# Second mixture, layer two: copies of the first two products moved ahead of operand halves on ScalarE, and one sum ahead of a low part on VectorE

## The chip, the cores and the metric

One core of a Trainium2 chip runs the whole program in one launch. The metric is device time in microseconds (us). An engine here is TensorE (PE in the rows), its weight load (PEld), VectorE (DVE), ScalarE (ACT), GpSimd (POOL) or SyncE (SP). The kernel was run three times; the profile below is of a further execution.

## The reference, cut to what matters

Attention within clusters feeds a first feed-forward block, and its output x (1536 tokens by 512) goes into a mixture of eight experts. The change touches only the mixture:

```python
logits = x @ w_gate
logits = logits - logits.max()
P = np.exp(logits)
for _ in range(8):
    P /= P.sum(1, keepdims=True) + 1e-09
    P /= P.sum(0, keepdims=True) + 1e-09
    P *= N / E
out = np.zeros((N, D), dtype=np.float32)
for e in range(E):
    h = np.maximum(x @ w1[e], 0.0)
    ye = h @ w2[e]
    out += P[:, e:e + 1] * ye
```

N is 1536, D 512, E 8, and w1[e] is 512 by 1024.

## The kernel before, in words

**Blocks and stages.** The mixture runs as 16 blocks `s`: each expert's 1024 hidden columns are two blocks of 512. A block has 14 stages `i` (`n = 14 * s + i`): stages 0 to 6 are layer one (x by w1), stages 7 to 13 layer two (h by w2). Each layer is a 2 by 2 block product written as seven smaller products with sums of blocks as operands (Strassen's scheme in a form of Winograd's). The products of layer two come in the order 1, 5, 6, 3, 7, 2, 4 (`order`), one per stage, so product 1 is stage 7, product 5 stage 8, product 6 stage 9, product 3 stage 10. From block 1 on, two of layer one's products are done as quarters (`quad`), and those of the second are interleaved with product 1 in stage 7.

**Operands.** Every float32 operand is split in a high part (`wfh`, `ah`; rounded by ScalarE, L863 and L1078) and a low part (`wfl`, `al`; the difference, by VectorE, L750), and each product is three matmuls: high by high, low by high, high by low. An operand of layer two has two halves of 128 by 768, k = 0 and 1: `h_hi(s, p, k)` and `h_lo(s, p, k)` make `ah` and `al` of product p. A product is 36 matmuls of 256 columns, first the 18 of half 0, then the 18 of half 1, and it fills three banks of PSUM, each with two columns of 256. The inputs of the halves are sums that VectorE makes in place: `h_s2` (L1174) for product 6, `h_s3` (L1182) for product 3, `h_s4` (L747) for product 7.

**Banks and copies.** Products 1, 6, 7 and 4 add up in one set of three banks (`b_1`), products 5 and 3 in another (`b_5`), product 2 in a third. After each product ScalarE copies all three banks out, scaled by the share of the expert (`evacuate_b`, six ACTIVATEs of L1137 per product; three plain copies, L1134, for expert 0). So product 6 may write a bank only when product 1 has been copied out of it, and product 3 only when product 5 has. The copy goes to one of four places in SBUF (`stage`, taken in turn), and GpSimd issues a DMA that adds it to the output in HBM (L1146). A place is free again when the DMA of four copies earlier has landed; and the DMAs of products 6 and 3 add to the same part of the output, so that of product 3 is issued when that of product 6 has landed.

**What sets the order.** The mixture runs under `tc.manual_schedule`: on TensorE, VectorE, ScalarE and GpSimd instructions stand in the order in which the Python loop emits them. At the head of stage n the loop copies out the product of stage n - 1. A half k = 1 is made at the head of the next stage (`LATES`), a half k = 0 in the stage before its product.

Of the kernel before, what the change touches and what calls it, by code (L numbers as in the profile page):

```python
# [38 lines left out]
def attention_moe_kernel(ctx, tc, kq, vp, cent, w_in, w_out, w_gate, w1, w2, out):  # L39
# [11 lines left out]
    def r(t):  # L51
        return t.bitcast(F32)
# [393 lines left out]
    with tc.manual_schedule(engines={ENG.PE, ENG.DVE, ENG.Activation, ENG.Pool, ENG.SP}):  # L446
# [147 lines left out]
        for pair in range(-4, NPAIR + 4):  # L594
            for item in ORDER:
                kind, at, *place = item.split(",")
                f, stride, low, high = KINDS[kind]
                i = int(at) + stride * pair
# [243 lines left out]
    def factor_lo(n, e):  # L842
        if n in ready:
            x, hi, lo = ready[n]
            lo_of(e, lo, x, hi)
            ready[n] = (hi, lo)
# [180 lines left out]
    def quad_add(s, q, four=False):  # L1027
        m, h = QAT[q]
        t = hb[s, "21" if four else "11"][:, m, h * CH : (h + 1) * CH]
        tt(vec, t, qbanks[s, four][QB[q]][:, :CH], t, ALU.add)  # L1030
# [11 lines left out]
    def half_product(ps, groups, k, which, opened):  # L1042
        for u, cols, lf, rt in groups[which]:
            for q, (i, j) in enumerate(((0, 0), (0, 1), (1, 0))):
                nc.tensor.matmul(ps[u][:, cols], lhsT=lf(i, k), rhs=rt(j, k), start=u not in opened, stop=k == 1 and q == 2, skip_group_check=True)  # L1045
                opened.add(u)
# [34 lines left out]
    def h_lo(s, p, k, relu=False):  # L1081
        (hi,) = hf[s, p, k]
        x = hb[s, PLACE[p]][:, k]
        lo = ahp.tile([P, HT], F32R, name=f"al{p}_{s}_{k}", tag="al")
        if relu:
            vec.scalar_tensor_tensor(out=lo, in0=x, scalar=0.0, in1=r(hi), op0=ALU.max, op1=ALU.subtract)
        else:
            lo_of(vec, lo, x, hi)
        hf[s, p, k].append(lo)
# [20 lines left out]
    def evacuate_b(n, banks=(0, 1, 2)):  # L1110

        s, i = divmod(n, 14)
        p, ps, e = order(n)[i - 7], psn[n], s // (F2 // FB)
        i, j = GOES[p]
        if s == NS - 1 and p in (3, 7, 2, 4):

            t = kept[i, j]
            for u in banks:
                for m in (2 * u, 2 * u + 1):
                    vec.scalar_tensor_tensor(out=t[:, m], in0=two_(ps[u])[:, m % 2], scalar=Pg[:, 6 * i + m, e : e + 1], in1=t[:, m], op0=ALU.mult, op1=ALU.add)  # L1120
                part = slice(2 * u, 2 * u + 2)
                if p != 3:
                    for m in (4, 5) if p == 4 and u == 2 else (part,):
                        stores[0] += 1
                        (nc.sync, nc.scalar)[stores[0] % 2].dma_start(out=out_block(i, j)[:, m], in_=t[:, m])
                else:
                    gps.dma_start(out=out_block(i, j)[:, part], in_=t[:, part], accum_op=ALU.add)
            return
        t = stage()
        kept[i, j] = t  # L1130
        for u in range(3):
            z = two_(ps[u])
            if e == 0:
                act.copy(t[:, 2 * u : 2 * u + 2], z)  # L1134
                continue
            for m in range(2):
                act.mul(t[:, 2 * u + m], z[:, m], Pg[:, 6 * i + 2 * u + m, e : e + 1])  # L1137
        if s == NS - 1:
            if p in (1, 5):
                gps.dma_start(out=t, in_=out_block(i, j), accum_op=ALU.add)  # L1140
            return
        to = out_block(i, j, first_out if e == 0 else out)
        if s in (0, F2 // FB) and p in (1, 6, 5, 4):
            nc.sync.dma_start(out=to, in_=t)
        else:
            gps.dma_start(out=to, in_=t, accum_op=ALU.add)  # L1146
# [23 lines left out]
    def h_s2(s, ks=(0, 1)):  # L1170

        for k in ks:
            h = hb[s, "11"][:, k]
            vec.scalar_tensor_tensor(out=h, in0=h, scalar=0.0, in1=hb[s, "12"][:, k], op0=ALU.max, op1=ALU.subtract, reverse1=True)  # L1174
# [19 lines left out]
    for s in range(NS1):  # L1194
        n = 2 * s + 1
# [54 lines left out]
    s = NS1 - 1  # L1250
# [76 lines left out]
    with tc.manual_schedule(engines={ENG.PE, ENG.DVE, ENG.Activation, ENG.Pool}):  # L1327
        psn = {}
        for n in range(14 * NS + 1):
            s, i = divmod(n, 14)  # L1330

            late = LATES.get(i - 1)
            ends = s == NS - 1
            if ends and i == 11:
                evacuate_b(n - 1, (0, 1))
                h_lo(s, 2, 0, True)
                factor_lo(n + 1, vec)
            if late:
                h_hi(s, late, 1, late == 2)
                h_lo(s, late, 1, late == 2)  # L1340
# [4 lines left out]
            if i == 5:  # L1345
                factor_hi(n + 3)
                if s == 0:
                    h_hi(s, 1, 0, relu=True)
                    h_hi(s, 1, 1, relu=True)
            if i == 2 or i == 7 and s:  # L1350
                pass
            elif n and i <= 7 and i > 0:
                evacuate_a(n - 1)
            elif n:
                evacuate_b(n - 1, (2,) if ends and i == 11 else (0, 1, 2))
# [72 lines left out]
            if i == 9:  # L1428
                h_s4(s)
            late = LATES.get(i)  # L1430
            if late and i > 7:
                h_hi(s, late, 0, late == 2)
                if not ends or late != 2:
                    h_lo(s, late, 0, late == 2)
# [17 lines left out]
            if i == 0:  # L1452
                g = groups1(n, ready.pop(n), xf[1])
                sets[n // 7, 1] = [ps3.tile([P, 512], F32, name=f"a{s}_1_{u}", tag="s") for u in range(3)]
                psn[n] = psn[n + 2] = sets[n // 7, 1]
                multiply(psn[n], g[:2], True)
                quad(s, 1)
                multiply(psn[n], g[2:], True)
                quad(s, 2)
            elif i == 1:  # L1460
                g = groups1(n + 1, ready.pop(n + 1), xf[6])
                quad(s, 5)
                multiply(psn[n + 1], g[:1], False)
                quad(s, 6)
                multiply(psn[n + 1], g[1:2], False)
                quad_add(s, 5)
                quad_add(s, 6)
                if 0 < s < 3:
                    route(1)
                if s == 0:  # L1470
                    x_sum((0, 0), t2, (0, 0), (0,))
            elif i == 2:
                quad(s, 7)
                multiply(psn[n], g[2:3], False)
                quad(s, 3)
                multiply(psn[n], g[3:], False)
                quad_add(s, 7)
                if 0 < s < 3:
                    route(1)
                if s == 0:  # L1480
                    x_sum((0, 0), t2, (0, 0), (1,))
                quad(s, 4)
                quad_add(s, 3)
                if 0 < s < 3:
                    route(1)
                if s == 0:
                    x_factor(7, (0, 0), (0,))
                quad_add(s, 4)
                ready.pop(n - 1)
                factor(n + 2, vec)  # L1490
                if s == 0:
                    x_factor(7, (0, 0), (1,))
                    x_factor(3, (1, 1))
                w_sums1(n + 5, vec)
            elif i == 6:
                if s == 0:
                    psn[n] = whole4(s, n)
            elif i < 7:
                psn[n] = product(n, groups1(n, ready.pop(n), xf[p]))
            elif i == 7 and s:  # L1500
                for q in (2, 1, 5):
                    quad(s, q, True)
                g = groups2([hf.pop((s, p, k)) for k in range(2)], ready.pop(n))
                psn[n] = sets[n // 7, 1] = [ps3.tile([P, 512], F32, name=f"b{s}_1_{u}", tag="s") for u in range(3)]
                opened = set()
                half_product(psn[n], g, 0, slice(0, 6), opened)
                quad_add(s, 2, True)
                quad_add(s, 1, True)
                quad_add(s, 5, True)
                h_s1(s, (1,))  # L1510
                h_hi(s, 5, 1)
                quad(s, 6, True)
                quad(s, 3, True)
                half_product(psn[n], g, 1, slice(0, 3), opened)
                quad_add(s, 6, True)
                h_lo(s, 5, 0)
                factor_hi(n + 2)
                quad_add(s, 3, True)
                quad(s, 7, True)
                half_product(psn[n], g, 1, slice(3, 6), opened)  # L1520
                quad_add(s, 7, True)
                factor_lo(n + 2, vec)
                h_s2(s, (0,))
                h_hi(s, 6, 0)
                quad(s, 4, True)
                ready.pop(n - 1)
                quad_add(s, 4, True)
                h_lo(s, 5, 1)
                h_lo(s, 6, 0)
                h_s2(s, (1,))  # L1530
            else:
                psn[n] = product(n, groups2([hf.pop((s, p, k)) for k in range(2)], ready.pop(n)), by_half=n < 14 * NS - 1)
            psn.pop(n - 3, None)
# [41 lines left out]
```

## Time and profile before

| | |
|---|---|
| median of three runs | 1471.24 us (1468.68 to 1471.83) |
| the profiled execution's own time | 1465.42 us |
| its span in the profile | 1463.6 us |
| granted TensorE clock, mean | 0.999 |
| PE busy | 1428.2 us (98%) |
| PE weight load busy | 1286.6 us (88%) |
| VectorE busy | 1180.7 us (81%) |
| ScalarE busy | 984.9 us (67%) |
| GpSimd busy | 363.4 us (25%) |

How to read it: matmuls overlap in the pipeline, so the busy time of PE is not its peak, and the time from one matmul's start to the next one's tells more. A line of a group of instructions shows the tile written, an arrow, and the tiles read. A bracket at the end of a line tells how long the engine stood idle before it and what released it. "b<-wfh,ah" at L652 is a matmul of layer two, at L1045 one of product 1; "a<-" is layer one; "q" and "r" are the quarters.

### The profile page before, as it was taken

The numbers are of one execution on the slowest core, as the hardware profiler recorded it, in microseconds if no ns is written. First come the engines' busy times: TensorE is split into PE (matmuls) and PEld (weight loads), VectorE is DVE, ScalarE is ACT, GpSimd is POOL, SyncE is SP. The second block draws the span as 40 slices with busy tenths as digits, with TensorE's granted clock in tenths as the row PEclk, the third lists the DMA queues.
The fourth block names the chain that finished last, engine by engine and source line by source line (L and its number), as shares of the span: only waits on it lengthen the run. The fifth ranks groups of instructions, "written<-read, shape, count | busy, mean of one in ns | idle before, by whom it ended". The sixth has DMA issues, their size and how long they took to land.

```text
span 1463.6 us, 25345 instructions
## 1 busy us (share of the span) xinstructions
PE 1428.2 (98%) x9703; PEld 1286.6 (88%) x9704; DVE 1180.7 (81%) x1977; ACT 984.9 (67%) x1900; POOL 363.4 (25%) x357
## 2 busy tenths in 40 slices
PE   8999999999999999999999999999999999999998
PEld 5777777888888899999999999899998998989998
DVE  7788888678788999897787877878778787787878
ACT  7677677663745575667758677586775866758664
POOL 6677752112120000203122221121111211112111
PEclk9999999999999999999999999999999999999999
DMA  7666521121130144849688797685956958569586
GB/s 220 184 167 167 158 64 58 46 71 61 55 102 30 30 118 92 146 107 200 104 159 143 139 200 117 116 147 95 177 94 116 157 96 166 95 115 161 96 155 130
DMA packets 136315, 177.49 MB, mean 121 GB/s; under 512 B 6273, under 2 KB 108673, under 8 KB 136193
## 3 DMA queue, kind: packets, MB, share of 16 engines
q0 software_dynamic: 83584, 87.30, 39.4%
q1 hardware_dynamic: 51104, 87.32, 19.5%
q8 instruction: 76, 1.25, 0.3%
q10 hardware_dynamic: 1504, 1.25, 0.3%
q14 instruction: 47, 0.38, 0.1%
HBM read 65.36 MB, written 88.87 MB: 105 GB/s over the span
## 4 chain that ended last, share of the span: by engine, by line
PE 26%; DVE 9%; DMA 8%; ACT 5%; issue 2%; ACTq 0%; DVEq 0%
PE a L652 12%; DMA out_dram<-acc 8%; PE b L652 7%; ACT acc L1137 3%; PE b L1045 3%; PE r L1025 3%; DVE h L747 2%; PE q L1025 2%; DVE al L750 2%; DVE h L1174 1%; ACT ah L1078 1%; DVE wfl L750 1%; DVE w0r L747 1%; DVE qs L747 1%; DVE acc L1120 1%
## 5 line engine op out<-in xcount | busy, mean ns | idle before, releaser
L652 PE MATMUL b<-wfh,ah 128*128 128x256 f32 x1164 | 331.7, 285 | 14.3 <-ACT acc L1137 13.6
L652 PE MATMUL b<-wfh,al 128*128 128x256 f32 x1164 | 329.2, 283 | 0.0
L652 PE MATMUL b<-wfl,ah 128*128 128x256 f32 x1164 | 329.1, 283 | 0.0
L1146 POOL DMA_DIRECT2D out_dram<-acc x87 | 126.6, 1973 | 579.4 <-ACT acc L1137 579.4
L652 PEld LDWEIGHTS b<-wfh,ah 128*128 128x128 f32 x1164 | 222.8, 191 | 17.5 <-ACT acc L1137 16.4
L1078 ACT CAST ah<-h 128x768 fp32r<-128x768 f32 x160 | 136.6, 854 | 136.8 <-DVE h L1174 79.3
L1137 ACT ACTIVATE acc<-b,Pg 128x256 f32<-128x256 f32 x564 | 219.9, 525 | 12.8 <-DMA out_dram<-acc 12.8
L652 PEld LDWEIGHTS b<-wfl,ah 128*128 128x128 f32 x1164 | 223.1, 192 | 0.0
L652 PEld LDWEIGHTS b<-wfh,al 128*128 128x128 f32 x1164 | 223.0, 192 | 0.0
L652 PE MATMUL a<-xfh,wfh 128*128 128x512 f32 (+1 forms) x640 | 216.3, 338 | 0.1
L652 PE MATMUL a<-xfl,wfh 128*128 128x512 f32 (+1 forms) x640 | 215.7, 337 | 0.0
L652 PE MATMUL a<-xfh,wfl 128*128 128x512 f32 (+1 forms) x640 | 215.4, 337 | 0.0
L750 DVE TENSOR_TENSOR al<-h,ah 128x768 fp32r<-128x768 f32 x160 | 151.3, 954 | 43.3 <-ACT ah L1078 41.3
L1065 ACT COPY h<-a 128x512 f32<-128x512 f32 x192 | 110.3, 600 | 99.6 <-PE a L652 94.6
L652 PEld LDWEIGHTS a<-xfh,wfl 128*128 128x128 f32 x640 | 120.9, 189 | 13.0
L652 PEld LDWEIGHTS a<-xfh,wfh 128*128 128x128 f32 x640 | 121.1, 189 | 12.1 <-issue 0.6
L652 PEld LDWEIGHTS a<-xfl,wfh 128*128 128x128 f32 x640 | 121.1, 189 | 10.3
L313 ACT ACTIVATE p<-s,m 128x768 f32<-128x768 f32 x96 | 86.5, 903 | 39.4 <-DVE m L304 36.9
L304 DVE TENSOR_REDUCE m<-s 128x1 f32<-128x768 f32 x96 | 89.9, 951 | 13.4 <-PE s L297 13.1
L323 POOL TENSOR_SCALAR p<-p,rec 128x768 f32<-128x768 f32 x96 | 86.4, 912 | 48.7 <-DVE rec L318 41.4
L111 POOL TENSOR_TENSOR wr<-wr,u 128x512 f32<-128x512 f32 x32 | 44.3, 1384 | 183.2 <-DVE u L110 122.4
L747 DVE TENSOR_TENSOR h<-q,h 128x384 f32<-128x384 f32 x112 | 60.9, 554 | 35.2 <-PE q L1025 32.9
(258 smaller groups left out, 3370.7 us busy)
## 6 DMA issues: line engine op xcount, KB each, us to landing
out_dram<-acc POOLq DMA_DIRECT2D x91, 768.0 KB, 11.4
w0r<-in_w_dram SPq DMA_DIRECT2D x16, 1024.0 KB, 7.4
w1r<-in_w_dram SPq DMA_DIRECT2D x16, 1024.0 KB, 9.7
qk<-qk SPq DMA_DIRECT2D x45, 192.0 KB, 3.5
wr<-in_w_in_dram SPq DMA_DIRECT2D x16, 512.0 KB, 3.7
wr<-in_w_out_dram SPq DMA_DIRECT2D x16, 512.0 KB, 3.5
first_out<-acc POOLq DMA_DIRECT2D x10, 768.0 KB, 9.4
raw<-in_kq_dram SPq DMA_DIRECT2D x16, 384.0 KB, 4.5
```

What stands on the lines that cost most here:

```text
L111: wp0=lambda: nc.gpsimd.tensor_tensor(out=b, in0=b, in1=u(), op=ALU.mult),
L304: nc.vector.tensor_reduce(out=m, in_=tiles[i]["s"][:, :S], axis=AX.X, op=ALU.max, negate=True)
L313: nc.scalar.activation(t["p"], t.pop("s")[:, :S], AF.Exp, bias=t.pop("m"), accum_out=chunks[c]["sum"][:, j, 0:1])
L323: nc.gpsimd.tensor_scalar(out=p, in0=p, scalar1=chunks[c]["rec"][:, j : j + 1], scalar2=1.0, op0=ALU.mult, op1=ALU.mult)
L652: nc.tensor.matmul(ps[u][:, cols], lhsT=lf(i, k), rhs=rt(j, k), start=fresh and u not in opened, stop=k == 1 and q == 2, skip_group_check= ...
L747: e.tensor_tensor(out=out, in0=in0, in1=in1, op=op)
L750: e.tensor_tensor(out=lo, in0=x, in1=r(hi), op=ALU.subtract)
L1025: nc.tensor.matmul(ps, lhsT=quad_lhs(s, q, a, four), rhs=(x4 if four else xq)[b][:, XQ[q]], start=j == 0 and q in (1, 2, 5), stop=j == 2, ...
L1065: act.copy(bank(t, u), ps[u])
L1078: act.copy(hi, x)
L1137: act.mul(t[:, 2 * u + m], z[:, m], Pg[:, 6 * i + 2 * u + m, e : e + 1])
L1146: gps.dma_start(out=to, in_=t, accum_op=ALU.add)
```

## The change

The diff:

```diff
@@ -1335,6 +1335,10 @@
                 evacuate_b(n - 1, (0, 1))
                 h_lo(s, 2, 0, True)
                 factor_lo(n + 1, vec)
+            if i == 9 and s:
+                evacuate_b(n - 1)
+                h_hi(s, 3, 0)
+                h_lo(s, 3, 0)
             if late:
                 h_hi(s, late, 1, late == 2)
                 h_lo(s, late, 1, late == 2)
@@ -1347,7 +1351,7 @@
-            if i == 2 or i == 7 and s:
+            if i == 2 or i in (7, 8, 9) and s:
                 pass
@@ -1428,7 +1432,7 @@
             late = LATES.get(i)
-            if late and i > 7:
+            if late and i > 7 + (s > 0):
                 h_hi(s, late, 0, late == 2)
@@ -1518,6 +1522,7 @@
                 quad_add(s, 3, True)
                 quad(s, 7, True)
                 half_product(psn[n], g, 1, slice(3, 6), opened)
+                evacuate_b(n)
                 quad_add(s, 7, True)
                 factor_lo(n + 2, vec)
                 h_s2(s, (0,))
@@ -1526,8 +1531,8 @@
                 quad_add(s, 4, True)
                 h_lo(s, 5, 1)
+                h_s2(s, (1,))
                 h_lo(s, 6, 0)
-                h_s2(s, (1,))
```

In blocks 1 to 15, the copies of product 1 move from the head of stage 8 into stage 7, ahead of the high halves of product 6. The copies of product 5 stay at the head of stage 9, but both halves of product 3 now stand behind them (half 0 stood ahead, in stage 8). The second `h_s2` moves ahead of the low half 0 of product 6. No instruction is added or taken out. The order on TensorE and SyncE is as before, and on GpSimd too. What moves is on ScalarE and VectorE; block 6 stands for all of blocks 1 to 15. In the names below the first number is the product (for `b`, `h`, `acc` and `wfh` see above), the second number the block for `ah` and `al`, and the third the half: `ah6_6_0` is product 6, block 6, half 0. `b6_1_0` is block 6, product 1, bank 0.

ScalarE in block 6, from the last weight cast of stage 7 on, before:

```order
L863 CAST wfh93_9880<-ws91_9684 128x512
L1078 CAST ah6_6_0_9899<-h11_6_9624 128x768
L1078 CAST ah6_6_1_9910<-h11_6_9624 128x768
L1137 ACTIVATE acc1_3475<-b6_1_0_9835,Pg_5397 128x256 x2
L1137 ACTIVATE acc1_3475<-b6_1_1_9836,Pg_5397 128x256 x2
L1137 ACTIVATE acc1_3475<-b6_1_2_9837,Pg_5397 128x256 x2
L1078 CAST ah3_6_0_9923<-h12_6_9687 128x768
L863 CAST wfh94_9927<-w1r6_9467 128x512
L1078 CAST ah3_6_1_9970<-h12_6_9687 128x768
L1137 ACTIVATE acc1_3475<-b6_5_0_9931,Pg_5397 128x256 x2
L1137 ACTIVATE acc1_3475<-b6_5_1_9932,Pg_5397 128x256 x2
L1137 ACTIVATE acc1_3475<-b6_5_2_9933,Pg_5397 128x256 x2
```

The same place with the change:

```order
L863 CAST wfh93_9880<-ws91_9684 128x512
L1137 ACTIVATE acc1_3475<-b6_1_0_9835,Pg_5397 128x256 x2
L1137 ACTIVATE acc1_3475<-b6_1_1_9836,Pg_5397 128x256 x2
L1137 ACTIVATE acc1_3475<-b6_1_2_9837,Pg_5397 128x256 x2
L1078 CAST ah6_6_0_9906<-h11_6_9624 128x768
L1078 CAST ah6_6_1_9917<-h11_6_9624 128x768
L863 CAST wfh94_9923<-w1r6_9467 128x512
L1137 ACTIVATE acc1_3475<-b6_5_0_9927,Pg_5397 128x256 x2
L1137 ACTIVATE acc1_3475<-b6_5_1_9928,Pg_5397 128x256 x2
L1137 ACTIVATE acc1_3475<-b6_5_2_9929,Pg_5397 128x256 x2
L1078 CAST ah3_6_0_9973<-h12_6_9687 128x768
L1078 CAST ah3_6_1_9977<-h12_6_9687 128x768
```

Product 1's six copies now stand ahead of both high halves of product 6, and product 5's six ahead of both high halves of product 3; the weight cast for product 3 (`wfh94`) stands ahead of product 5's copies.

VectorE at the same place, from the first `h_s2` on, before:

```order
L1174 SCALAR_TENSOR_TENSOR h11_6_9624<-h11_6_9624,h12_6_9687 128x768
L747 TENSOR_TENSOR h21_6_9779<-r6_2_9825,h21_6_9779 128x384
L750 TENSOR_TENSOR al5_6_1_9905<-h12_6_9687,ah5_6_1_9860 128x768
L750 TENSOR_TENSOR al6_6_0_9907<-h11_6_9624,ah6_6_0_9899 128x768
L1174 SCALAR_TENSOR_TENSOR h11_6_9624<-h11_6_9624,h12_6_9687 128x768
L750 TENSOR_TENSOR al6_6_1_9912<-h11_6_9624,ah6_6_1_9910 128x768
L1182 SCALAR_TENSOR_TENSOR h12_6_9687<-h21_6_9779,h11_6_9624 128x768 x2
L750 TENSOR_TENSOR al3_6_0_9925<-h12_6_9687,ah3_6_0_9923 128x768
L750 TENSOR_TENSOR wfl94_9928<-w1r6_9467,wfh94_9927 128x512
L750 TENSOR_TENSOR al3_6_1_9972<-h12_6_9687,ah3_6_1_9970 128x768
L747 TENSOR_TENSOR h11_6_9624<-h22_6_9732,h11_6_9624 128x768 x2
```

With the change:

```order
L1174 SCALAR_TENSOR_TENSOR h11_6_9624<-h11_6_9624,h12_6_9687 128x768
L747 TENSOR_TENSOR h21_6_9779<-r6_2_9825,h21_6_9779 128x384
L750 TENSOR_TENSOR al5_6_1_9912<-h12_6_9687,ah5_6_1_9860 128x768
L1174 SCALAR_TENSOR_TENSOR h11_6_9624<-h11_6_9624,h12_6_9687 128x768
L750 TENSOR_TENSOR al6_6_0_9915<-h11_6_9624,ah6_6_0_9906 128x768
L750 TENSOR_TENSOR al6_6_1_9919<-h11_6_9624,ah6_6_1_9917 128x768
L1182 SCALAR_TENSOR_TENSOR h12_6_9687<-h21_6_9779,h11_6_9624 128x768 x2
L750 TENSOR_TENSOR wfl94_9924<-w1r6_9467,wfh94_9923 128x512
L750 TENSOR_TENSOR al3_6_0_9975<-h12_6_9687,ah3_6_0_9973 128x768
L750 TENSOR_TENSOR al3_6_1_9979<-h12_6_9687,ah3_6_1_9977 128x768
L747 TENSOR_TENSOR h11_6_9624<-h22_6_9732,h11_6_9624 128x768 x2
```

The second `h_s2` has changed places with `al6_6_0`, and the low weight part `wfl94` with `al3_6_0`; the rest of the block is as it was.

## Rows read from the trace of the kernel before

**Rows 1.** Waits of PE over the whole span: total us, times, longest us
```profile
PE b L652 <- ACT acc L1137: 13.6, 14, 1.0
PE q L1025 <- DVE h L747: 6.2, 15, 0.5
...
PE b L652 <- ACT acc L1134: 0.7, 1, 0.7
```

**Rows 2.** Timeline of PE in block 6: start us, us, instruction [idle before]
```profile
884.75 0.28 PE L1045 MATMUL b<-wfh,al 128*128 128x256 f32 x1
...
885.40 0.28 PE L652 MATMUL b<-wfh,ah 128*128 128x256 f32 x1
...
889.58 0.28 PE L652 MATMUL b<-wfh,al 128*128 128x256 f32 x1
890.83 0.39 PE L652 MATMUL b<-wfh,ah 128*128 128x256 f32 x1 [0.97 <-ACT acc L1137]
891.05 0.28 PE L652 MATMUL b<-wfl,ah 128*128 128x256 f32 x1
```

**Rows 3.** Timeline of ACT in block 6
```profile
886.13 0.83 ACT L1078 CAST ah<-h 128x768 fp32r<-128x768 f32 x1 [2.75 <-DVE h L1174]
889.21 0.83 ACT L1078 CAST ah<-h 128x768 fp32r<-128x768 f32 x1 [2.24 <-DVE h L1174]
889.94 2.30 ACT L1137 ACTIVATE acc<-b,Pg 128x256 f32<-128x256 f32 x6
892.10 0.86 ACT L1078 CAST ah<-h 128x768 fp32r<-128x768 f32 x1
...
896.40 0.83 ACT L1078 CAST ah<-h 128x768 fp32r<-128x768 f32 x1
897.14 0.61 ACT L863 CAST wfh<-w1r 128x512 fp32r<-128x512 f32 x1
897.66 0.83 ACT L1078 CAST ah<-h 128x768 fp32r<-128x768 f32 x1
898.40 2.29 ACT L1137 ACTIVATE acc<-b,Pg 128x256 f32<-128x256 f32 x6
...
913.69 2.31 ACT L1137 ACTIVATE acc<-b,Pg 128x256 f32<-128x256 f32 x6 [1.42 <-DMA out_dram<-acc]
```

**Rows 4.** Timeline of DVE in block 6
```profile
885.07 0.95 DVE L1174 SCALAR_TENSOR_TENSOR h<-h,h 128x768 f32<-128x768 f32 x1
...
886.41 1.81 DVE L750 TENSOR_TENSOR al<-h,ah 128x768 fp32r<-128x768 f32 x2
888.14 0.95 DVE L1174 SCALAR_TENSOR_TENSOR h<-h,h 128x768 f32<-128x768 f32 x1
890.07 0.96 DVE L750 TENSOR_TENSOR al<-h,ah 128x768 fp32r<-128x768 f32 x1 [0.97 <-ACT ah L1078]
890.95 1.82 DVE L1182 SCALAR_TENSOR_TENSOR h<-h,h 128x768 f32<-128x768 f32 x2
893.00 0.96 DVE L750 TENSOR_TENSOR al<-h,ah 128x768 fp32r<-128x768 f32 x1 [0.23 <-ACT ah L1078]
...
894.47 0.95 DVE L750 TENSOR_TENSOR al<-h,ah 128x768 fp32r<-128x768 f32 x1
895.35 1.82 DVE L747 TENSOR_TENSOR h<-h,h 128x768 f32<-128x768 f32 x2
```

**Rows 5.** Chain that ended last, one link in block 6: start us, us, what
```profile
901.14 12.45 DMA out_dram<-acc
```

**Rows 6.** Stretches: length, then PE, PEld, DVE, ACT, POOL busy; clock; DMA share; GB/s
```profile
886.30:892.60 6.30, 5.33 (x44) 5.13 (x43) 5.33 (x7) 4.06 (x9) 0.00 (x0) 1.00 0.01 3
892.60:913.60 21.00, 21.00 (x173) 20.83 (x172) 15.45 (x23) 19.67 (x44) 4.34 (x3) 1.00 0.96 163
912.55:925.90 13.35, 12.59 (x72) 10.88 (x71) 8.59 (x20) 7.44 (x16) 5.84 (x4) 1.00 0.88 129
1337.95:1350.13 12.18, 12.18 (x72) 10.97 (x70) 8.59 (x20) 7.39 (x16) 5.86 (x4) 1.00 0.96 141
```

**Rows 7.** Timeline of ACT in block 13, the copies of product 4
```profile
1337.90 2.30 ACT L1137 ACTIVATE acc<-b,Pg 128x256 f32<-128x256 f32 x6 [0.24 <-DMA out_dram<-acc]
```

## The prediction

> **What bounds the kernel now.** I read first the busy times in the table above: PE is busy 1428.2 of 1463.6 us, so a gain can only be PE's idle time. Second, who PE waits for [rows 1]: two waits return in nearly every block, 15 of a matmul of layer two for ScalarE's copies (13.6 + 0.7 us), and 15 of a quarter of layer one for VectorE's adds (6.2 us). Third, the timeline of one block for the three engines [rows 2 to 4]. Product 1's last matmul starts at 884.75 and ends at 885.03; product 5 runs from 885.40 to its last start at 889.58, so a matmul starts every 4.18/35 = 0.119 us; product 6 then starts only at 890.83 [rows 2]. The six copies of product 1 are what it waits for, and they start at 889.94 though their data were there from 885.03, because on ScalarE they stand behind the second high half of product 6, which itself waited 2.24 us for the second `h_s2` [rows 3]. That sum stands on VectorE behind a low half and starts at 888.14 [rows 4].
>
> What one wait costs: from 889.58 to 890.83 are 1.25 us instead of 0.12, which is 1.13, and the next matmul follows after 0.22 instead of 0.12; together 1.23 us, that is 0.26 more than the idle 0.97 of the row [rows 2]. Fourteen such and one shorter one (0.7 idle, so 0.96) are 18.2 us. The 15 waits for VectorE have 6.2/15 = 0.41 idle each; with the same 0.26 they are 0.67 each, 10.1 us. So 28.3 us at most.
>
> **The change, step by step in block 6.** Nothing is added; I move the rows by their own durations.
>
> *Product 1's copies.* ScalarE idles 2.75 us before 886.13 [rows 3], so copies fit there: one of a pair per (892.10 - 889.94)/6 = 0.36 us. The first two banks are full before the last, whose matmuls end at 885.03, so the last pair ends near 886.0. Even if all six started after 885.1 they would let ScalarE go at 885.1 + 2.16 = 887.26, which delays no step below. First cost: nothing, hidden by ScalarE's idle 2.75 us.
>
> *The second `h_s2`* goes from 888.14 to 886.41 + 0.87 = 887.28 and ends at 888.23, so the second high half of product 6 starts at 888.35 instead of 889.21 (the 0.12 between sum and cast is that of the rows). The price is that the low half 0 of product 6 starts at 888.15 instead of 887.28 and ends at 889.11. Product 6 wants it at its third matmul, 889.70 + 0.24 = 889.94: hidden, with 0.8 to spare.
>
> *VectorE behind it.* The second low half starts at 889.18 + 0.03 = 889.21 instead of 890.07, the `h_s3` pair at 890.09, the low weight part for product 3 at 891.83, and VectorE is free at 892.43.
>
> *Product 5's copies ahead of product 3's halves.* On ScalarE the weight cast follows at 889.09 and the copies at 889.61, with product 5's last matmul ending at 889.86, so no bank keeps them waiting for long. Product 3's high halves start at 889.61 + 2.16 = 891.77 and 892.51, its low ones at 892.63 and 893.50, which end at 893.59 and 894.46. Product 3 starts at 889.70 + 36 × 0.12 = 894.02 and wants the low half 0 at 894.26: hidden, 0.67 to spare.
>
> *Product 7.* `h_s4` starts at 894.38 instead of 895.35, its first half ends at 895.33; the high half of product 7 starts at 895.43 instead of 896.40, and by the spacing of rows 3 (0.74, 0.52, 0.74) product 6's copies start at 897.43 instead of 898.40: 0.97 earlier. PE follows 0.89 after the first copy's start (890.83 - 889.94), so at 898.32; product 7 would come to its banks at 894.02 + 4.32 = 898.34. This is tight. I charge 0.1 us a block, 1.5 us in all.
>
> *The stores.* GpSimd issues product 1's store some 6 us earlier. In the old order the DMA engines stood at a share of 0.01 from 886.30 to 892.60, and then at 0.96 until 913.60 [rows 6]. In these 21 us they moved the stores of products 1, 5 and 6 and a weight load; product 6's store alone took 12.45 us, from 901.14 to 913.59 [rows 5], and product 4's copies, the last ones of the block, waited 1.42 us for it [rows 3]. Product 1's store now falls into the idle 6.3 us, so some 5 us of work are out of the way ahead of product 6's store, and I put its landing at 909; the bounds are 908 (all of the 6 us saved) and 900.17 + 12.45 = 912.6 (issued 0.97 earlier, no faster). ScalarE comes to product 4's copies at 913.69 - 1.42 - 0.97 = 911.30. So this wait is gone at 909, and 1.3 us of it are left at 912.6.
>
> The rule for a queue in the Trainium skill ("PSUM — Partial Sum Buffer", section "Engine vs sequencer instructions") speaks against the change: ScalarE's and VectorE's queues are strictly first in, first out, so whatever waits inside six copies is also waited for by the halves behind them. The trace agrees, since product 1's copies stood behind a half from 885.03 to 889.94; by the rule the new order loses where a copy waits long, which is the last rival.
>
> *The quarters.* Without the 1.42 us, ScalarE starts on the next block's weights and first copies 1.42 + 0.97 = 2.39 us earlier, PE 1.13 (1.23 less the 0.1), so ScalarE, and VectorE which follows it there, gain 1.26 us on PE, more than the 0.67 of a wait. Block 13 shows the effect already: there product 4's copies waited 0.24 us only [rows 7], and the same 72 matmuls took 12.18 us, with PE busy throughout, instead of 13.35 in block 6 [rows 6]. I take nine tenths of the 10.1 us, 9.1.
>
> **The sum.** 18.2 - 1.5 + 9.1 = 25.8 us. From the profiled execution's 1465.42 this gives 1439.6. That execution lies 5.8 us below the median of the runs, 1471.24; the median becomes 1445.4, and I say 1445.
>
> **The rivals.**
>
> *A, the store still holds the block.* Product 6's store keeps its 12.45 us, because the weight load runs beside it anyway. Then product 4's copies start 0.97 earlier than now while PE could be 1.13 earlier; the quarters' wait grows, and a block gains 0.97: 15 × 0.97 = 14.6, so 1456.7. For it: the DMA engines are at 0.96 up to the landing. Against: their idle 6.3 us just before [rows 6]. It decides if the landing is later than 911.3.
>
> The page "DMA: Bandwidth & Descriptors" of the Trainium skill, section "Queues, rings and completion order", says that each DMA engine goes round-robin between the queues with work, a packet at a time; by that, the weight load slows the store from its own issue on whatever was moved before, which is rival A's mechanism. No row here separates the two queues.
>
> *B, the tight place gives way.* If ScalarE and VectorE gain nothing behind `h_s3` (a wait in between as long as the one removed), product 6's copies stay at 898.40, product 7 waits until 899.29, 0.95 later than it could start, and a block keeps 0.28 of its 1.23. With the quarters this is 15 × 0.28 + 9.1 = 13.3, so 1458. For it: a margin of 0.02 us. Against: every step is spaced as in the rows.
>
> *C, nothing moves.* If product 6 has another wait that ends at the same time. Its low half 1, which started at 890.07 [rows 4], is wanted only from 889.70 + 18 × 0.12 on, and high half 0 was there at 886.96, so little speaks for it: 1471.
>
> *D, slower.* The place in SBUF for product 1's copies is not free when they come to ScalarE's head. Then both halves of product 6 stand behind them, and everything after. They may start as late as 888.35 - 0.73 - 2.16 = 885.46 at no cost; 0.97 + 0.67 later, from 887.1 on, a block is slower than before. Starting at 889.94 as now, product 6's first high half would come at 892.10 and end at 892.96, and product 6 3.3 us after 889.70 instead of 1.13: 15 × 2.17 more, 1504. Against: the store that frees this place is four copies back, in the block before, and the DMA engines stand idle from 886.30 on [rows 6], so that every store has landed by then, ahead of the 887.1 that decides.
>
> **How the numbers follow.** A measurement of this kernel can tell 0.2%, some 3 us, from no change. Forecast 0.66, with its own range from 1441 (all 28.3 back, less 2 for the spread of the runs) to 1450; A 0.14; B 0.10; C 0.05; D 0.05. Faster is the forecast, A and B: 0.90; same 0.05; slower 0.05. The range goes from 1440 to 1458 and takes in A and B.
>
> **What would show it.** In the new profile the wait of layer two's matmuls for L1137 should be gone from PE's list, product 1's copies should end near 886.0 on a clock in which product 5 starts at 885.40, and product 6 should follow product 5 at 0.12. Product 4's copies should show no wait for a DMA, and the waits of the quarters should fall from 6.2 us to under 1. A wait of product 7's first matmul for ScalarE longer than 0.3 us is B; a DMA wait above 0.5 us before product 4's copies is A; a DMA wait before product 1's copies is D. A span above 1455 would make the forecast wrong.

## The result and the profile after

The changed kernel took 1437.67 us (median of 4 runs, 1437.05 to 1439.27) against 1470.53 before (now four runs); the ratio is 0.9779, 95% interval 0.9762 to 0.9796. That is 32.9 us faster; 25.8 were forecast, and the time lies 2.3 us below the low end of the range.

The first lines and the chain on the page of the changed kernel, and the median time of its stores at the page's end:

```profile
span 1435.3 us, 25375 instructions
...
PE 1420.8 (99%) x9703; PEld 1288.0 (90%) x9704; DVE 1181.7 (82%) x1977; ACT 986.3 (69%) x1900; POOL 366.5 (26%) x357
...
PE 74%; DVE 4%; ACT 3%; issue 1%; DVEq 0%; ACTq 0%
...
out_dram<-acc POOLq DMA_DIRECT2D x91, 768.0 KB, 8.9
```

PE is busy 99% of a shorter span, and the median store takes 8.9 us from issue to landing (11.4 before). The chain that ended last holds no DMA any more; before, DMA had 8% of the span in it ([rows 5] are one link). PE's list of waits over the whole span of the changed kernel, the longest of it:

```profile
PE oht L567 <- DVE oh L560: 1.5, 2, 1.1
PE t L332 <- POOL p L323: 1.5, 3, 0.7
PE wps L465 <- DVE wm L460: 1.5, 1, 1.5
```

All three lines of [rows 1] are gone, and what is left lies in the stages ahead of the mixture. Block 6 on PE (start, length, instruction): product 1's last matmul, product 5's first, product 6's first, product 7's first with its neighbours:

```profile
876.73 0.28 PE L1045 MATMUL b<-wfh,al 128*128 128x256 f32 x1
...
877.38 0.28 PE L652 MATMUL b<-wfh,ah 128*128 128x256 f32 x1
...
881.56 0.28 PE L652 MATMUL b<-wfh,al 128*128 128x256 f32 x1
881.68 0.28 PE L652 MATMUL b<-wfh,ah 128*128 128x256 f32 x1
...
890.20 0.28 PE L652 MATMUL b<-wfh,al 128*128 128x256 f32 x1
890.32 0.36 PE L652 MATMUL b<-wfh,ah 128*128 128x256 f32 x1
890.52 0.28 PE L652 MATMUL b<-wfl,ah 128*128 128x256 f32 x1
```

Product 6 follows product 5 after 0.12 us where 1.25 stood before [rows 2]. Product 5's start is 8.02 us earlier on this clock than in the profile before (885.40 there), so 8.02 added to a time here lets it be read against the prediction's. ScalarE in block 6 (same columns):

```profile
875.27 0.83 ACT L1137 ACTIVATE acc<-b,Pg 128x256 f32<-128x256 f32 x2
876.34 1.57 ACT L1137 ACTIVATE acc<-b,Pg 128x256 f32<-128x256 f32 x4 [0.23 <-PE b L1045]
878.10 0.84 ACT L1078 CAST ah<-h 128x768 fp32r<-128x768 f32 x1 [0.19 <-DVE h L1174]
880.30 0.83 ACT L1078 CAST ah<-h 128x768 fp32r<-128x768 f32 x1 [1.36 <-DVE h L1174]
881.04 0.62 ACT L863 CAST wfh<-w1r 128x512 fp32r<-128x512 f32 x1
881.56 2.29 ACT L1137 ACTIVATE acc<-b,Pg 128x256 f32<-128x256 f32 x6
883.71 1.59 ACT L1078 CAST ah<-h 128x768 fp32r<-128x768 f32 x2
887.41 0.83 ACT L1078 CAST ah<-h 128x768 fp32r<-128x768 f32 x1 [2.10 <-DVE h L747]
...
889.40 2.29 ACT L1137 ACTIVATE acc<-b,Pg 128x256 f32<-128x256 f32 x6
...
902.97 2.48 ACT L1137 ACTIVATE acc<-b,Pg 128x256 f32<-128x256 f32 x6
```

These answer to [rows 3]. With 8.02 added: product 1's copies end at 877.91, so at 885.93 (forecast: near 886.0); product 6's second half starts at 888.32 (888.35), product 5's copies at 889.58 (889.61), product 7's half at 895.43 (895.43), product 6's copies at 897.42 (897.43). Product 4's copies, the last row, have no bracket for a DMA any more. The stores of products 1, 5, 6 and 3 from GpSimd's timeline, and the stretch of layer one that answers to [rows 6]:

```profile
878.27 1.45 POOL L1146 DMA_DIRECT2D out_dram<-acc  x1 [7.83 <-ACT acc L1137]
884.20 1.43 POOL L1146 DMA_DIRECT2D out_dram<-acc  x1 [4.49 <-ACT acc L1137]
892.14 1.46 POOL L1146 DMA_DIRECT2D out_dram<-acc  x1 [6.50 <-ACT acc L1137]
902.67 5.84 POOL L1146 DMA_DIRECT2D out_dram<-acc  x4 [9.07 <-DMA out_dram<-acc]
```

```profile
903.37:915.45 12.08, 12.08 (x72) 11.05 (x71) 8.76 (x20) 7.22 (x16) 5.13 (x4) 1.00 1.07 157
```

Product 3's store goes out as soon as product 6's has landed, so that landing is just ahead of 902.67; by the trace it comes 9.9 us after the issue at 892.14 (12.45 before [rows 5]), at about 902.1. The 72 matmuls that took 13.35 us in this block before take 12.08, with PE busy throughout.

### The profile page after: what moved, and what is told of

It is laid out like the page before. It is cut to its first block, busy times and chain, and to the rows that moved or that the text cites. A ratio compares the mean times of both kernels' runs of the same rounds, so it can differ in the third digit from the quotient of the medians.

```text
span 1435.3 us, 25375 instructions
## 1 busy us (share of the span) xinstructions
PE 1420.8 (99%) x9703; PEld 1288.0 (90%) x9704; DVE 1181.7 (82%) x1977; ACT 986.3 (69%) x1900; POOL 366.5 (26%) x357
## 3 DMA queue, kind: packets, MB, share of 16 engines
q8 instruction: 76, 1.25, 0.4%
q10 hardware_dynamic: 1504, 1.25, 0.3%
## 4 chain that ended last, share of the span: by engine, by line
PE 74%; DVE 4%; ACT 3%; issue 1%; DVEq 0%; ACTq 0%
PE b L652 27%; PE a L652 23%; PE y L706 9%; PE b L1045 4%; PE q L1025 4%; PE r L1025 4%; PE l L652 3%; DVE acc L1120 1%; ACT h L674 1%; DVE h L678 1%; DVE al L750 0%; ACT gh L688 0%; ACT h L683 0%; DVE vl L139 0%; PE a L1039 0%
## 5 line engine op out<-in xcount | busy, mean ns | idle before, releaser
L1065 ACT COPY h<-a 128x512 f32<-128x512 f32 x192 | 113.4, 618 | 101.8 <-PE a L652 96.8
L652 PEld LDWEIGHTS a<-xfh,wfh 128*128 128x128 f32 x640 | 121.2, 189 | 11.9 <-issue 0.6
L304 DVE TENSOR_REDUCE m<-s 128x1 f32<-128x768 f32 x96 | 90.0, 951 | 13.5 <-PE s L297 13.2
```

The lines of the kernel that those rows point to most:

```text
L304: nc.vector.tensor_reduce(out=m, in_=tiles[i]["s"][:, :S], axis=AX.X, op=ALU.max, negate=True)
L1065: act.copy(bank(t, u), ps[u])
```

## The experiments

Three parts of the change alone or left out, two experiments on the store, and further profiles of both kernels. Ratios are to the kernel before on the same chip.

### sum_only

```diff
+                h_s2(s, (1,))
                 h_lo(s, 6, 0)
-                h_s2(s, (1,))
```

> Only the second h_s2 ahead of the low half 0 of product 6; the copies stay where they were. Theory (two separate waits: product 6's belongs to the order of sum, halves and copies, the quarters' to the landing of product 6's store): by the rows, the sum at 887.28 lets product 1's copies start 0.86 us earlier, so product 6 loses 0.3 to 0.4 us a block instead of 1.23; product 6's store is issued 0.9 us earlier too, but is no faster, so the quarters' waits stay at 6 us or more. Time 1470.5 - 13 = 1457. Rival (the copies' place alone makes product 6 wait): still about 1 us a block, time above 1466.

Measured: 1457.2 us, ratio 0.9909 (0.9891 to 0.9926). PE's list over the span, and the copies' wait for a DMA in ScalarE's list:

```profile
PE q L1025 <- DVE h L747: 7.7, 18, 0.5
```

```profile
ACT acc L1137 <- DMA out_dram<-acc: 14.8, 11, 2.4
```

The last line reads in the kernel before:

```profile
ACT acc L1137 <- DMA out_dram<-acc: 12.8, 12, 1.7
```

The wait of layer two is off the list, the quarters' is not, and the DMA wait is about as it was. In block 6 product 6's first matmul comes 0.38 after product 5's last (884.79 to 885.17), so 0.26 is lost instead of 1.13:

```profile
884.79 0.28 PE L652 MATMUL b<-wfh,al 128*128 128x256 f32 x1
885.17 0.38 PE L652 MATMUL b<-wfh,ah 128*128 128x256 f32 x1
```

So moving one line on VectorE takes away most of product 6's wait with the copies left in their place, and the quarters wait for something else.

### copies_only

```diff
-            if i == 2 or i == 7 and s:
+            if i == 2 or i in (7, 8) and s:
                 pass
...
                 half_product(psn[n], g, 1, slice(3, 6), opened)
+                evacuate_b(n)
```

> Only product 1's copies ahead of product 6's high halves; sum and product 5's copies stay as before. Theory: product 6 no longer waits, but the chain of sum, halves and h_s3 is as late as before, product 5's copies start at about 894.0 as before, and product 3 comes 1.1 us earlier: the wait goes over to product 3, 0.9 us a block, so 15 x 0.3 = 4 us; product 1's store is 6 us earlier, so the quarters' waits go (10 us). Time 1452 to 1456. Rival (moving the copies is the whole gain): no wait at product 3, time 1438 to 1442.

Measured: 1455.82 us, ratio 0.9906 (0.9881 to 0.9930). PE's waits, then the one in block 6:

```profile
PE b L652 <- ACT acc L1137: 9.6, 14, 0.7
...
PE q L1025 <- DVE h L747: 1.3, 3, 0.5
```

```profile
891.63 0.38 PE L652 MATMUL b<-wfh,ah 128*128 128x256 f32 x1 [0.69 <-ACT acc L1137]
```

In this run product 5 starts at 882.16, so two products later is 882.16 + 2 × 4.31 = 890.78: the wait has gone to product 3, 0.85 us, as expected. The quarters are nearly free: three waits are left. So moving the copies alone ends product 6's wait too, but hands it on; moving the sum hands on little of it.

### change_less_sum

```diff
                 h_lo(s, 5, 1)
-                h_s2(s, (1,))
                 h_lo(s, 6, 0)
+                h_s2(s, (1,))
```

(against the changed kernel)

> The change without the moved sum. Theory: the chain sum, high half, low half, h_s3, h_s4 is as late as before, so product 6's copies start at about 898.3 and product 7, which comes 0.8 us earlier, waits 0.7 to 0.9 us a block; the quarters' waits are gone. Time 1450 to 1455. Rival (the sum matters little once the copies are out): under 0.2 us a block, time under 1442.

Measured: 1450.93 us, ratio 0.9866 (0.9850 to 0.9882). PE in block 6, product 3's third matmul and product 7's first with the ones before them:

```profile
892.06 0.28 PE L652 MATMUL b<-wfl,ah 128*128 128x256 f32 x1
892.43 0.39 PE L652 MATMUL b<-wfh,al 128*128 128x256 f32 x1
...
896.48 0.28 PE L652 MATMUL b<-wfh,al 128*128 128x256 f32 x1
897.11 0.39 PE L652 MATMUL b<-wfh,ah 128*128 128x256 f32 x1 [0.34 <-ACT acc L1137]
```

Product 3 loses 0.25 for its low half, product 7 0.51; together with the slower restarts that is the 0.7 to 0.9 expected at product 7 alone. The chain behind the sum was as late as before, and the waits moved along it.

### copies_and_sum

```diff
-            if i == 9 and s:
-                evacuate_b(n - 1)
-                h_hi(s, 3, 0)
-                h_lo(s, 3, 0)
...
-            if i == 2 or i in (7, 8, 9) and s:
+            if i == 2 or i in (7, 8) and s:
...
-            if late and i > 7 + (s > 0):
+            if late and i > 7:
```

(against the changed kernel)

> The change without its middle part: product 3's halves stay around the weight cast, ahead of product 5's copies. Theory: product 5's copies start near 893.1, and product 3 comes at 894.0 to banks that are free 0.9 us after that: no wait or under 0.1 us a block; same time as the change, 1437 to 1440. Rival (the halves behind product 5's copies are needed): a wait of product 3 of 0.3 us a block or more, time above 1442.

Measured: 1444.88 us, ratio 0.9822 (0.9804 to 0.9840), some 7 us more than the change. This was missed. Product 3 does not wait, as expected, but the quarters do; then GpSimd's stores of products 1, 5 and 6 in block 6:

```profile
PE q L1025 <- DVE h L747: 2.8, 8, 0.5
```

```profile
881.27 1.45 POOL L1146 DMA_DIRECT2D out_dram<-acc  x1 [7.75 <-ACT acc L1137]
890.75 1.43 POOL L1146 DMA_DIRECT2D out_dram<-acc  x1 [8.03 <-ACT acc L1137]
895.11 1.46 POOL L1146 DMA_DIRECT2D out_dram<-acc  x1 [2.93 <-ACT acc L1137]
```

Without the middle part product 5's store stands 4.36 us ahead of product 6's; with it 7.94 (884.20 and 892.14 above), so that it hardly runs into product 6's any more. In block 6 product 5's store takes 7.3 us here and lands 2.9 us after product 6's is issued; with the middle part it takes 7.5 us and lands 0.5 us ahead of it. The middle part buys nothing on PE in layer two (the table below); it spaces two stores.

### middle_only

```diff
+            if i == 9 and s:
+                evacuate_b(n - 1)
+                h_hi(s, 3, 0)
+                h_lo(s, 3, 0)
...
-            if i == 2 or i == 7 and s:
+            if i == 2 or i in (7, 9) and s:
...
-            if late and i > 7:
+            if late and i > 7 + (s > 0):
```

> Only the middle part: product 5's copies ahead of both halves of product 3; product 1's copies and the sum as before. Theory (this part pays only because the other two make room): by the rows of before, product 5's copies go from 894.07 to 892.62, the high half 0 of product 3 from 892.10 to 894.78 and its low half to 895.65, where product 3 at 895.15 wants it by 895.39: product 3 waits 1.2 us a block and product 7 some 0.6, so 15 x 1.8 = 27 us slower, less what the quarters get back (up to 10): 1478 to 1495. Rival (it helps by itself, through product 5's earlier store): 1465 or less.

Measured: 1482.3 us, ratio 1.0077 (1.0062 to 1.0092): slower. PE in block 6 at product 3:

```profile
901.53 0.28 PE L652 MATMUL b<-wfh,al 128*128 128x256 f32 x1
902.11 0.39 PE L652 MATMUL b<-wfh,ah 128*128 128x256 f32 x1 [0.30 <-ACT ah L1078]
902.33 0.28 PE L652 MATMUL b<-wfl,ah 128*128 128x256 f32 x1
903.10 0.39 PE L652 MATMUL b<-wfh,al 128*128 128x256 f32 x1 [0.49 <-DVE al L750]
```

Product 3 waits for its high half (0.58 instead of 0.12) and for its low half (0.77), as worked out. Its list has no wait of a quarter and ScalarE's none for a DMA, although product 1's store goes out where it did before: product 5's stands 7.8 to 7.9 us ahead of product 6's here too. A part that is worth 7 us on top of the other two costs 11 by itself.

### late_store

```diff
+        elif p == 1:
+            held.append((to, t))
         else:
             gps.dma_start(out=to, in_=t, accum_op=ALU.add)
+            while held:
+                to, t = held.pop()
+                gps.dma_start(out=to, in_=t, accum_op=ALU.add)
```

(against the changed kernel, in `evacuate_b`)

> The change, but GpSimd issues product 1's store behind product 5's, some 6 us later, so that the DMA engines stand idle again before it. Theory (the quarters wait because product 6's store lands late): product 6's store takes 12 us again, product 4's copies wait 1 us or more for it, the quarters' waits are back (6 us or more in PE's list), product 6 still does not wait: 1454 to 1458. Rival (the quarters' waits went because ScalarE was freed by the new order, not by the store): no wait of the quarters, 1437 to 1441.

Measured: 1454.37 us, ratio 0.9885 (0.9870 to 0.9899). PE's list, and the copies' in ScalarE's:

```profile
PE q L1025 <- DVE h L747: 7.3, 17, 0.5
```

```profile
ACT acc L1137 <- DMA out_dram<-acc: 14.6, 11, 3.0
```

The order on ScalarE, VectorE and PE is that of the change, and the copies are as early; only the DMA is later, and both waits are back. In block 6 product 6's store takes 12.0 us where the change has 9.9. So the quarters' wait is the store's, and rival A's mechanism with its price (1456.7 forecast) is real; the change escapes it because the stores of products 1 and 5 are nearly out of the way when product 6's is issued.

### no_store_1

```diff
-        else:
+        elif p != 1 or s < 3:
             gps.dma_start(out=to, in_=t, accum_op=ALU.add)
```

(against the kernel before, in `evacuate_b`)

> The kernel before without product 1's store from block 3 to 14 (its copies stay; the output lacks product 1's part of these blocks). Theory: product 6's store lands some 4 us earlier, the DMA wait of product 4's copies and the quarters' waits go (10 us), product 6 still loses 1.23 us a block: 1456 to 1460. Rival (these waits hang on the same chain as product 6's wait): the quarters still wait, 1467 or more.

Measured: 1457.52 us, ratio 0.9913 (0.9893 to 0.9934).

```profile
PE b L652 <- ACT acc L1137: 13.6, 14, 1.0
...
PE q L1025 <- DVE h L747: 0.9, 3, 0.5
```

The converse: product 6's wait is to the tenth that of [rows 1], the quarters' is nearly gone, with three waits left. The two waits are separate.

### before_again, before_third and after_again

No edit.

> The kernel before once more, for a second profile and the spread of its runs. The profiled execution of before was 5 us below the median of its runs, that of the change is at its median. Theory (the waits for the store vary from execution to execution, and vanish with the change): an execution of 1470 us shows the quarters' waits or the DMA wait of product 4's copies larger than the 6.2 and 12.8 us of the first profile by several us in sum. Rival (the clock): the waits are the same, and the granted clock lies 0.3% lower.

> The kernel before a third time, one profile. Theory (what differs between its executions are the waits behind product 6's store): its span above 1435.3 is the sum of product 6's 18 us and what layer one of the blocks loses, so an execution near 1470 shows 8 us or more for the quarters, one near 1465 about 6. Rival (the clock): 6.2 us whatever the time.

> The change once more. Theory (PE is the bound, nothing in the mixture waits for a store): 1437 to 1439, no wait of layer two or of a quarter above 0.5 us in PE's list, and a spread of the runs of 3 us or less. Rival (the first profile was a lucky execution, as that of before was): waits of 3 us or more come back.

Measured: before_again 1470.31 us (11 runs, 1467.73 to 1473.22; its profile is of an execution of 1470.31), before_third 1474.44 (one execution), after_again 1438.16 (4 runs, 1437.35 to 1438.73; ratio 0.9778, 0.9762 to 0.9794). PE's waits in before_again, then in before_third, there with ScalarE's:

```profile
PE b L652 <- ACT acc L1137: 13.6, 14, 1.0
PE q L1025 <- DVE h L747: 8.3, 19, 0.5
```

```profile
PE b L652 <- ACT acc L1137: 13.6, 14, 1.0
PE q L1025 <- DVE h L747: 9.5, 22, 0.5
```

```profile
ACT acc L1137 <- DMA out_dram<-acc: 20.2, 12, 2.5
```

Over three executions of 1465.42, 1470.31 and 1474.44 us product 6's wait does not move, while the quarters wait 15, 19 and 22 times for 6.2, 8.3 and 9.5 us, and the copies' own wait for the store is 12.8, 13.5 and 20.2 us. The whole loss is read from PE's stretches: "layer two" is here from the start of product 5's first matmul to the start of product 4's last, summed over the blocks (in block 0 from product 1's first), and "layer one" is what lies between these stretches, product 1 included. Before_again's layer one is 4.7 us longer than the first profile's, of 4.9 us in the span. In before_third it is 7.5 of 9.0 us; most of the rest, 1.9 us, lies ahead of the mixture's layer two, where the granted clock of its first 20 us is 0.91 (1.00 in the other two). The clock (0.999 and 1.000) does not tell the first two profiles apart.

The same stretches for every run, with product 6's store in blocks 3 to 14: how long ahead of it product 5's store is issued, and how long it takes itself from issue to landing (shortest, median, longest):

| run | layer two, us | layer one, us | product 5's store ahead, us | product 6's store, us | blocks in which it lands too late for product 4's copies |
|---|---|---|---|---|---|
| before | 436.5 | 502.8 | 4.2 to 4.4 | 11.4, 12.1, 12.7 | 12 of 12 |
| before_again | 436.5 | 507.5 | 4.2 to 4.4 | 9.9, 12.8, 13.1 | 11 |
| before_third | 436.5 | 510.3 | 4.2 to 4.4 | 11.9, 12.7, 13.5 | 12 |
| sum_only | 423.4 | 506.9 | 4.2 to 4.4 | 11.4, 12.6, 13.5 | 12 |
| copies_only | 432.3 | 494.6 | 4.2 to 4.4 | 9.6, 11.1, 12.0 | 6 |
| no_store_1 | 436.5 | 493.6 | 4.2 to 4.4 | 9.6, 10.6, 12.5 | 3 |
| copies_and_sum | 419.6 | 497.6 | 4.2 to 4.4 | 9.8, 11.3, 12.3 | 8 |
| late_store | 419.7 | 507.0 | 7.8 to 7.9, product 1's right behind it | 11.2, 12.2, 14.1 | 11 |
| middle_only | 463.9 | 491.6 | 7.8 to 7.9 | 8.0, 9.0, 10.2 | 0 |
| change_less_sum | 432.3 | 491.6 | 7.8 to 7.9 | 8.0, 8.8, 10.1 | 0 |
| after | 419.6 | 491.6 | 7.8 to 7.9 | 8.2, 8.9, 9.9 | 0 |
| after_again | 419.5 | 491.7 | 7.8 to 7.9 | 8.0, 8.8, 9.6 | 0 |

In all of them ScalarE comes to product 4's copies 10.8 to 11.2 us after product 6's store is issued. A store that takes longer holds them, and layer one is longer; where none does, layer one is 491.6 or 491.7 us.

The second profile of the changed kernel lists no wait of layer two or of a quarter.

## Why the prediction was right or wrong

**The bound and the two waits: right.** The gain came back at the two places named. From profile to profile PE's idle time fell from 35.4 to 14.5 us; the other 7.4 of the 28.3 us are busy time (1428.2 to 1420.8), which answers to the slow restarts that the prediction charged at 0.26 a wait. Layer two gave back 16.8 us, where 18.2 - 1.5 = 16.7 were forecast.

**The steps in block 6: right.** Each row of ScalarE falls within 0.04 us of its forecast start. Product 7's tight place held, with 0.20 instead of 0.12 after its first matmul, 0.08 a block where 0.1 was charged.

**The store: it landed early enough, but in good part for a reason that was not seen.** Product 6's store was put at a landing of 909; it lands at 902.1 + 8.02 = 910.1, ahead of product 4's copies at 902.97 + 8.02 = 910.99: 0.9 us to spare in block 6, where 911.30 - 909 = 2.3 were forecast. The prediction gave the saving to product 1's store alone and told nothing of product 5's, which goes out 4.5 us earlier, 3.5 of them because its copies stand ahead of product 3's halves (in copies_and_sum it is 1.0 earlier). The runs say that this counts for more: with product 1's store moved and product 5's still 4.2 to 4.4 us ahead of product 6's, the store lands too late in 6 blocks (copies_only) or 8 (copies_and_sum, 7 us missing); with product 1's left where it was and product 5's 7.8 us ahead, in none (middle_only). Taking product 1's store away altogether leaves 3 (no_store_1). That the forecast of this wait came out is to that extent luck.

**The quarters: under-sized.** Nine tenths of 10.1 us were counted; the whole wait went, and layer one gave back 502.8 - 491.6 = 11.2 us against the first profile. Nor was it one wait in nearly every block: the 15 waits follow 11 of the blocks, two in four of them, block 6 among these.

**The step that failed: "that execution lies 5.8 us below the median of the runs, 1471.24; the median becomes 1445.4".** The 5.8 us were carried over as if every kernel had them. They belonged to the kernel before: further waits behind product 6's store, of which other executions have more than the profiled one. The profile of before_again, an execution at the median, shows it: its layer one takes 507.5 us instead of 502.8, and the rest of the span is within 0.3 us of the first profile's. So the quarters' term, 9.1 us in the sum, was worth 507.5 - 491.6 = 15.9 us in an execution at the median. The change takes away the cause, so the changed kernel's profiled execution (1437.13) lies close to its median (1437.67); its runs spread 2.2 us (four runs) and 1.4 (four of after_again), those of before_again 5.5 (eleven). In spans, profile against profile, the gain is 1463.6 - 1435.3 = 28.3 us, the prediction's "at most"; the 4.6 us beyond come from this step. The low end of 1440 allowed 2 us of spread; without the 5.8 added it would have held the time.

**The rivals.** A did not come, but late_store makes it at 1454; B and C did not come. D's fear, halves late behind copies, is seen in middle_only, for product 3 and at a lower price (11 us). Of the two rules of the Trainium skill, first in, first out ("PSUM — Partial Sum Buffer", section "Engine vs sequencer instructions") is what the trace of middle_only agrees with: both waits of product 3 (0.58 and 0.77 us) are for halves behind copies. Whether the round-robin of the DMA queues ("DMA: Bandwidth & Descriptors", section "Queues, rings and completion order") sets the store's time no run here separates.

What makes the store's time differ from block to block and between executions of the same kernel stays open; the weight load beside it was not taken away, and its share was not tried.

## What to carry to other kernels

A wait that names one engine has a queue behind it: follow the queues back to the instruction whose operands were ready and that only stood in line, here a sum behind a low half, and copies behind a half. When a copy moves, its DMA moves with it, and when stores are spaced out, a wait two stages later may go. Before a gain from one profiled execution is taken to the median, ask whether the gap between the two is itself made of the waits that the change removes; here it was, in a kernel whose chain ran through DMA.

## What the runs showed that was not expected

The parts do not add up: 13 us (sum_only), 15 us (copies_only) and -11 us (middle_only) make 17, all three together 33: the middle part costs 27 us in layer two by itself and nothing behind the other two. And an execution's distance from the next one was not spread over the kernel: 4.9 us between the first two profiles of the kernel before (spans 1463.6 and 1468.5), with product 6's 14 waits equal to a tenth of a microsecond and the quarters' changed by four waits; 4.7 us of it are in layer one.
